# A bucketed attention with a Mish feed-forward layer on one core: float32 scores for the first 256 tokens alone, keys and values of the first head pairs in a buffer of their own, and a new order

## The chip, the core and the metric

The kernel runs on one core of a Trainium2 chip. The core has a matrix engine (PE, with its weight loads as PEld), a vector engine (DVE), a scalar engine (ACT), a general engine (POOL) and a queue engine (SP), which here issues every transfer. The engines run side by side, each through its own list of instructions in order, and wait for one another by semaphores. The metric is the device time of one execution in microseconds (us); less is better. A difference under about 0.3% (2.5 us) can't be told from none.

## The reference

For 4 batches of 8 heads, 768 tokens and 64 dimensions, queries and keys are hashed to 6 bits by the signs of a projection; a query attends only to keys of its own bucket. The 3,072 token rows of 512 channels then pass a feed-forward layer with h·tanh(softplus(h)).

```python
mask = q_bucket[:, :, :, None] == k_bucket[:, :, None, :]
scores = scale * np.matmul(q, k.transpose(0, 1, 3, 2))
scores = np.where(mask, scores, -1000000000.0)
attn = np.exp(scores - np.max(scores, axis=-1, keepdims=True))
attn = attn / (np.sum(attn, axis=-1, keepdims=True) + 1e-09)
...
h = x @ w_in
g = h * np.tanh(np.where(h > 20.0, h, np.log1p(np.exp(np.minimum(h, 20.0)))))
out = g @ w_out
```

The inputs of the feed-forward layer's weights are float64 and are brought to float32 on the chip from their bits.

## The kernel before

**Groups and slots.** The work is cut into 12 groups of 256 tokens (the code's `u`): batch 0 is groups 0, 1 and 2. A group has 8 slots (`n`), two for each of its 4 head pairs (`j`); a slot is 128 queries of a pair, both heads. A group also has 8 blocks `H`/`O` of the feed-forward layer. `BACKBONE` (L224) gives the order of the large steps on PE: S (scores of a slot), V (attention times values), H (first feed-forward product), O (second). The feed-forward layer runs three blocks of four slots behind the attention, so the first 12 slots stand largely before the first H.

**Two ways to a score.** In most slots the operands are float16 in two parts, high and low, with the hash bits beside the low part: `pe` (L933), 8 matmuls of float16 in a slot (line L937). This needs `q_prep` (L879) and `k_prep` (L786), which split a tensor (`k_hi`, `k_cp`, `k_lo` in the order's words), transpose both parts by a DMA through SP (L472), form hash bits with small PE products (L739), a sum (L743) and compares (L748). The other way is float32: `pe32` (L944, line L948) multiplies float32 halves on 64 rows each and adds bfloat16 hash bits. It needs `q_prep32` (L774) and `k_prep32` (L761): a transpose on PE (`turn32`, L450, with a copy at L453) and a product with the signed projection (`hash32`, L461, with a compare at L464). No DMA transpose and no splitting is needed for it.

**Who takes which.** `NF = 2` and `F32U = 3` (L219, L220): pairs 0 and 1 of groups 0, 1 and 2 take float32, that is 12 slots; the keys of pairs 0 and 1 of batch 0 are never split. All else takes float16. In group 0 the probabilities are transposed by PE (`pe_turn`, L434, copied by ACT at L437 or DVE at L438) and multiplied with raw float32 values (L1062), and its feed-forward blocks are float32 too (L1120, L1169).

**Memory.** The raw keys and values of batch 0 lie where other things will be: pairs 0 and 1 in the weights' tile `wi` (words 3072 to 6143), the values of pair 2 in the first slot of the ring `hl`, the keys of pairs 2 and 3 in `PT` (`kv_place`, L676). The ring `hl` holds normalised probabilities in two parts before their transposition. The weight pieces pass `w_prep` (conversion from float64 bits, L594 to L607) and `w_split` (into two float16 parts).

**What sets the order.** The operations are recorded in a plan, each with the engines that can do it; the table `ORDER` lists the plan's numbers with a letter for the engine chosen. Each engine's list is what falls to it from this table, so that a transfer that SP waits for holds up those behind it, and DVE, ACT and POOL do the softmax steps and the preparation steps in one fixed sequence: `max` at L978, scale at L961/L968, `exp` at L991, the row sum's reciprocal at L1021, `hi`/`lo` parts at L390 to L415.

Of the kernel before, what the change touches and what calls it, by code (L numbers as in the profile page):

```python
# [8 lines left out]
F16 = mybir.dt.float16  # L9
# [9 lines left out]
P = 128  # L19
# [8 lines left out]

# [59 lines left out]
137 7 9 8 50 20 0 5 11 19 12 22 1 2 3 4 76 80 29 81b 13 37 6 77b 14 15 10 25 33 26 30b 38 17 27 28 18 34 39 52  # L94
60 61 35 62 41 56 54 63 57 55 21 42 48 51 53 24 23 31 78 36 32 64 65 16 86 91 138 92 79 87 147 40 88 82 117 83
43 118 44 119b 93 89 66 109 110 111 153 90 94 120 67 112 154b 132 107d 46 108 133 113 95 115 68 114 116 124
125b 155 121 126 101 84 45 134 136 135 156 127b 178 96 128 140b 148 141 47 58 149 85 122d 123 97 99 142 139b
98b 143 129 168d 179 180d 100 174 176 69 175 177 170 130 157 171b 131 172 173b 204 205b 169 70 145b 182 189
144b 102 158 159 181 161b 190b 71 193 291 194 195 185 191 150 186 192 220 221 103 222d 183b 187 206 160b 196
188 197 104 223 212 152 146 49 151 162 59 105 106 213b 207 216 218 217b 219b 214 215b 184 353 224 243 163 239  # L100
164 244 245b 241 248 240 242 233c 270 368 307 210d 208 235 254 236 255 249 209b 237 246 238 247 225 256 271
250 257 234 272d 262 263 268 266 292 198 273 226 267b 211 227 293 165 294 269 251 283 284 349 350 264 303 265
285 295 166 304b 354 305 296 258 199 200 309d 286b 310 311c 260c 261 306 274 281 313 253 252 232 228 282 312b
322 201 317 364 287 365 288 289 290 366 318 319 355b 323 324 308 320 321 367 330b 331 315 338 339 72 231 203
202 167 229 397 369b 314 329 316 325 297 298b 275 276b 340 333 341 230 332b 334 342 73 370d 299 336 425c 277
74 426 371 399 378 379 380 335 328 302 400 398 300 373 424 423 351 337 301 280 381 427 372b 374 382 389c 411
376 259 375 278 279 406 429 458 428 390 412 452 407 352 391 383 384b 393 392c 395 326 327 385 453 408d 409 410
# [118 lines left out]

# [1119 lines left out]
```

## Time and profile before

| | us |
|---|---|
| median of 3 runs | 818.18 (816.49 to 818.43) |
| span of the profiled execution, first to last instruction | 815.4 |
| PE busy | 798.2 |
| DVE busy | 602.9 |
| ACT busy | 624.9 |
| POOL busy | 426.9 |

The span of the profiled execution lies 2.8 us under the median: a run's time has a start and an end around the span. The sums of the prediction are made on the span and carried to the median unchanged. [...]

### The profile page before, as it was taken

The page shows a single profiled execution, that of the slowest core. Times are in us where ns is not written, and L with a number is a line of the kernel's source. Part 1 is how long each engine was busy: PE and PEld are TensorE (multiplying, and loading weights), DVE is VectorE, ACT ScalarE, POOL GpSimd, SP SyncE. Part 2 cuts the span into 40 slices and gives each one's busy share as a digit, 9 for nine tenths or more (in the row PEclk, how much of TensorE's full clock was granted, in tenths as well). Part 3 has the DMA queues.
Part 4 walks back from the last instruction along what each step waited for, and adds up shares of the span by engine and source line. Part 5 has one row for each costly group of instructions (what it writes and reads, how often), then busy time and mean ns, then how long its engine had stood idle before and what let it go on. Part 6 is the DMA issues. An engine that isn't in the chain of part 4 may idle for free.

```text
span 815.4 us, 17000 instructions
## 1 busy us (share of the span) xinstructions
PE 798.2 (98%) x6546; PEld 549.6 (67%) x6546; DVE 602.9 (74%) x1103; ACT 624.9 (77%) x976; POOL 426.9 (52%) x434
## 2 busy tenths in 40 slices
PE   8899999999999999999999999999999999999998
PEld 5556666666676776676666676667676676776674
DVE  5888999988898778887887767768877675566211
ACT  4889998888696769889679698989779785677211
POOL 3564446554356773733585564344646758845120
PEclk9999999999999999999999999999999999999999
DMA  7958998989999969989989959999989577466200
GB/s 253 219 174 221 240 246 196 191 156 206 217 160 182 203 116 181 170 158 216 185 172 155 195 117 151 197 213 192 167 140 169 107 139 145 81 124 133 50 27 27
DMA packets 395489, 134.29 MB, mean 165 GB/s; under 512 B 365456, under 2 KB 386448, under 8 KB 395408
## 3 DMA queue, kind: packets, MB, share of 16 engines
q1 hardware_dynamic: 395408, 133.21, 81.2%
q8 instruction: 51, 0.84, 0.4%
q14 instruction: 30, 0.25, 0.1%
HBM read 35.65 MB, written 6.29 MB: 51 GB/s over the span
## 4 chain that ended last, share of the span: by engine, by line
PE 47%; ACT 1%; DVE 1%; DMA 1%; issue 0%; POOL 0%; SPq 0%; ACTq 0%; DVEq 0%
PE ps_s L937 7%; PE ps_o L1179 6%; PE ps_o L1181 6%; PE ps_o L1180 6%; PE ps_acc L1130 5%; PE ps_t L1088 5%; PE ps_acc L1132 5%; PE ps_acc L1131 5%; ACT pb L991 1%; DVE svb L978 1%; DMA out_dram<-ffb 1%; PE ps_t L739 0%; ACT L1315 0%; DVE hl L408 0%; ACT tok L480 0%
## 5 line engine op out<-in xcount | busy, mean ns | idle before, releaser
L991 ACT ACTIVATE pb<-ps_s,svb 128x768 f32<-128x768 f32 x184 | 180.9, 987 | 87.4 <-DVE svb L968 36.7
L978 DVE TENSOR_REDUCE svb<-ps_s 128x2 f32<-128x1536 f32 x92 | 161.3, 1753 | 40.2 <-PE ps_s L937 33.7
L1130 PE MATMUL ps_acc<-X,wo 128*128 128x256 f16 x616 | 167.9, 273 | 0.3 <-ACT ffb L1151 0.3
L1132 PE MATMUL ps_acc<-X,wo 128*128 128x256 f16 x616 | 167.9, 273 | 0.0
L1131 PE MATMUL ps_acc<-X,wo 128*128 128x256 f16 x616 | 167.9, 273 | 0.0
L1315 ACT ACT_TABLE_LOAD x117 | 150.1, 1283 | 2.0
L408 DVE SCALAR_TENSOR_TENSOR hl<-pb,svb,hl 128x768 f16<-128x768 f32 x131 | 140.3, 1078 | 13.8 <-POOL hl L390 9.8
L1181 PE MATMUL ps_o<-wi,ffb 128*128 128x512 f16 x352 | 133.4, 379 | 0.0
L1180 PE MATMUL ps_o<-wi,ffb 128*128 128x512 f16 x352 | 133.4, 379 | 0.0
L1179 PE MATMUL ps_o<-wi,ffb 128*128 128x512 f16 x352 | 133.4, 379 | 0.0
L937 PE MATMUL ps_s<-KT,QT 128*128 128x512 f16 (+1 forms) x656 | 120.1, 326 | 2.1 <-ACT pb L991 1.8
L390 POOL TENSOR_SCALAR hl<-pb,svb 128x768 f16<-128x768 f32 x68 | 71.0, 1046 | 75.9 <-DVE svb L1021 28.8
L937 PEld LDWEIGHTS <-QT 128*128 128x128 f16 x672 | 64.2, 98 | 40.5 <-issue 8.3
L1088 PE MATMUL ps_t<-PT,VT 128*64 128x256 f16 x1584 | 90.7, 273 | 0.0
L1088 PEld LDWEIGHTS <-VT 128*64 128x64 f16 x1584 | 84.8, 110 | 8.1 <-issue 7.6
L1151 ACT ACTIVATE ffb<-ps_acc,smalls 128x512 f32<-128x512 f32 x88 | 58.5, 684 | 33.5 <-PE ps_acc L1132 32.0
L415 POOL TENSOR_TENSOR hl<-pb,hl 128x768 f16<-128x768 f32 x45 | 75.0, 1667 | 3.8
L414 POOL TENSOR_SCALAR pb<-pb,svb 128x768 f32<-128x768 f32 x45 | 44.4, 987 | 48.0 <-ACT hl L392 21.4
L1131 PEld LDWEIGHTS <-wo 128*128 128x128 f16 x616 | 60.2, 98 | 13.3 <-issue 1.5
L1130 PEld LDWEIGHTS <-wo 128*128 128x128 f16 x616 | 60.2, 98 | 12.6 <-issue 0.5
L1132 PEld LDWEIGHTS <-wo 128*128 128x128 f16 x616 | 60.2, 98 | 7.0
L1181 PEld LDWEIGHTS <-ffb 128*128 128x128 f16 x352 | 34.4, 98 | 41.6
(240 smaller groups left out, 1300.5 us busy)
## 6 DMA issues: line engine op xcount, KB each, us to landing
out_dram<-ffb SPq DMA_DIRECT2D x22, 256.0 KB, 2.7
stg<-in_v_dram SPq DMA_DIRECT2D x13, 384.0 KB, 4.0
stg<-in_k_dram SPq DMA_DIRECT2D x12, 384.0 KB, 4.0
wo<-in_q_dram SPq DMA_DIRECT2D x9, 512.0 KB, 4.9
stg<-in_moe_w_in_dram SPq DMA_DIRECT2D x8, 512.0 KB, 4.6
stg<-in_moe_w_out_dram SPq DMA_DIRECT2D x6, 512.0 KB, 4.6
PT<-hl SPq DMA_TRANSPOSE x176, 4.1
wo<-in_moe_w_out_dram SPq DMA_DIRECT2D x5, 512.0 KB, 4.7
```

What stands on the lines that cost most here:

```text
L408: return [("DVE", 215 + 1.035 * n, port(lambda: nc.vector.scalar_tensor_tensor(out=dst, in0=src, scalar=sc, in1=hi, op0=ALU.mult, op1=ALU. ...
L937: nc.tensor.matmul(ps[:, hh * S + c0 * P:hh * S + c1 * P], QTb[:, u % 2, sl, qi], KTb[:, j, sl, hh * NCH + c0:hh * NCH + c1].rearrange("p ...
L978: op("max", [("DVE", 1755, lambda: nc.vector.tensor_reduce(out=sv[:, 0], in_=ps.rearrange("p (h e) -> p h e", e=S), axis=AX.X, op=ALU.max, ...
L991: EXP[n, hh] = op("exp", [("ACT", 1075, lambda hh=hh, t=t: nc.scalar.activation(pb[:, t], HOMES[n][0][:, hh * S:(hh + 1) * S], AF.Exp, bia ...
L1088: nc.tensor.matmul(pv[hh * D:(hh + 1) * D, y * 256:(y + 1) * 256], vt[:, w, hh * NCH + c], pt[:, hh, a * NCH + c].rearrange("p s t -> p (s ...
L1130: nc.tensor.matmul(o, wh, X[:, 0, c], start=(c == 0), stop=False)
L1131: nc.tensor.matmul(o, wh, X[:, 1, c], start=False, stop=False)
L1132: nc.tensor.matmul(o, wl, X[:, 0, c], start=False, stop=(c == NCC - 1))
L1179: nc.tensor.matmul(PS[f"o{s}"], gh, wh, start=first, stop=False)
L1180: nc.tensor.matmul(PS[f"o{s}"], gh, wl, start=False, stop=False)
L1181: nc.tensor.matmul(PS[f"o{s}"], gl, wh, start=False, stop=last)
L1315: for fn in plan.ordered("exp", lambda x: nc.scalar.preload_act_table_set(sets[x])):
```

## The change

`F32U` becomes 1: only group 0 takes float32 scores for its pairs 0 and 1 (4 slots instead of 12). So groups 1 and 2 drop `q_prep32`, and their `q_prep` takes all 16 blocks of 64 columns instead of 8. The keys of pairs 0 and 1 of batch 0 are now split as well: the two lines at L1241 that record `kv_stat(0, j, True)` and `k_prep(0, j)` at slots 1 and 3 come to life. Group 1 takes its pairs in the order 2, 3, 0, 1 (`turned`, L914). A new tile `ext` of 3,840 words holds the raw keys and values of pairs 0 and 1 and the values of pair 2; its room comes from the scratch for transfers, which is set to 1,024 bytes a partition. The tile `X` is laid out with the parts inside the channel blocks. The table `ORDER` is replaced as a whole: 2,655 operations instead of 2,636.

```diff
-F32U = 3
+F32U = 1
...
+    ext = cp.tile([P, 10 * S // 2], F32, name="ext")
...
-    Xb = ring("X", 2, [2, NCC, 256], F16)
+    Xb = ring("X", 2, [NCC, 2, 256], F16)
...
         if b == 0 and j < 2:
-            return [("wi", 3072 + (2 * j + x) * NKV, 3072 + (2 * j + x + 1) * NKV) for x in range(2)]
+            return [("ext", (2 * j + x) * NKV, (2 * j + x + 1) * NKV) for x in range(2)]
         if b == 0:
-            return [("pt1", (j - 2) * NKV, (j - 1) * NKV), ("hl", 0, NKV) if j == 2 else (SPARE[0], SPARE[1], SPARE[1] + NKV)]
+            return [("pt1", (j - 2) * NKV, (j - 1) * NKV), ("ext", 4 * NKV, 5 * NKV) if j == 2 else (SPARE[0], SPARE[1], SPARE[1] + NKV)]
...
-    nc = _bacc.Bacc("TRN2", target_bir_lowering=False, num_devices=1)
+    nc = _bacc.Bacc("TRN2", target_bir_lowering=False, num_devices=1, dynamic_dma_scratch_size=1024)
```

The first lines of the table, which say little by themselves:

```diff
-137 7 9 8 50 20 0 5 11 19 12 22 1 2 3 4 76 80 29 81b 13 37 6 77b 14 15 10 25 33 26 30b 38 17 27 28 18 34 39 52
...
+149 7 9 0 20 22 19 11 12 1 2 3 33 29 13 37 25 52 60 5 6 34b 18 30b 17 26b 10 14 35 38 15 27 61 36 62 54 50 31 28
```

PE at the first slot of group 1, before (ps_s: scores; QT, KT: transposed queries and keys; ps_l, ps_t: banks for transposes; X: raw queries):

```order
L948 LDWEIGHTS QT
L948 MATMUL ps_s<-KT,QT 128x512
L948 LDWEIGHTS QT
L948 MATMUL ps_s<-KT,QT 128x256
L948 LDWEIGHTS QT
L948 MATMUL ps_s<-KT,QT 128x256
L434 MATMUL ps_l<-ffb,pb 128x128 x3
L450 MATMUL ps_t<-ffb,X 64x128 x8
L434 MATMUL ps_l<-ffb,pb 128x128 x3
```

The same place on PE now (the line numbers of the changed kernel are 7 lower here; L930 is the float16 score, L427 the transpose of probabilities):

```order
L930 LDWEIGHTS QT
L930 MATMUL ps_s<-KT,QT 128x256
L930 LDWEIGHTS QT
L930 MATMUL ps_s<-KT,QT 128x512
L930 LDWEIGHTS QT
L930 MATMUL ps_s<-KT,QT 128x512
L427 MATMUL ps_l<-ffb,pb 128x128 x3
L427 MATMUL ps_t<-ffb,pb 128x128 x3
L427 MATMUL ps_l<-ffb,pb 128x128 x3
```

The score is float16, and the transposition of the next queries (L450) is gone from behind it.

DVE in group 0, around the fourth score maximum, before (svb: softmax scalars; hsum: hash sums; wo: where the split keys of pairs 2 and 3 stand before their transposition; PT: transposed probabilities):

```order
L743 TENSOR_REDUCE hsum<-ps_t 128x72
L748 TENSOR_SCALAR wo<-hsum 128x12x6
L743 TENSOR_REDUCE hsum<-ps_t 128x72
L978 TENSOR_REDUCE svb<-ps_b 128x2
L438 COPY PT<-ps_l 128x3x128 x2
```

The same stretch on DVE now (tok_64: where split keys or queries stand; L971 is the maximum, L386 and L401 the two parts of the split, L597 a part of the weights' conversion, L431 the copy of transposed probabilities):

```order
L386 TENSOR_SCALAR tok_64<-ext,smalls 128x12x64
L899 TENSOR_SCALAR smalls<-smalls 128x1
L401 SCALAR_TENSOR_TENSOR tok_64<-ext,smalls,tok_64 128x12x64
L736 TENSOR_REDUCE hsum<-ps_t 128x72
L431 COPY PT<-ps_l 128x3x128
L494 TENSOR_SCALAR smalls<-ps_t 128x4
L478 TENSOR_SCALAR smalls<-smalls 128x4
L971 TENSOR_REDUCE svb<-ps_b 128x2
L431 COPY PT<-ps_t 128x3x128
L597 TENSOR_SCALAR wi<-stg 128x1024
```

The split of a raw key tile from `ext` and a weight conversion stand between the softmax steps of group 0.

SP in group 0, before:

```order
L472 DMA_TRANSPOSE KT<-wo 128x12x128 x2
L472 DMA_TRANSPOSE QT<-tok_65 128x8x128
L468 DMA wi<-in_moe_w_in_dram 128x2x512
L472 DMA_TRANSPOSE KT<-wo 128x12x128
L468 DMA wo<-in_moe_w_in_dram 128x2x512
L472 DMA_TRANSPOSE KT<-wo 128x12x128
L468 DMA X<-in_q_dram 128x8x128
```

SP in the same place now:

```order
L465 DMA_TRANSPOSE KT<-wo 128x12x128
L465 DMA_TRANSPOSE QT<-tok_65 128x8x128
L465 DMA_TRANSPOSE KT<-tok_64 128x12x128
L465 DMA_TRANSPOSE KT<-wo 128x12x128
L461 DMA wo<-in_moe_w_in_dram 128x2x512
L465 DMA_TRANSPOSE KT<-tok_65 128x12x128
L461 DMA wi<-in_moe_w_in_dram 128x2x512
L465 DMA_TRANSPOSE KT<-wo 128x12x128
L465 DMA_TRANSPOSE QT<-tok_64 128x16x128
```

Two more key transposes (those of pair 0) stand among the others; those of pair 1 come later, among the transposes of `hl`.

## Rows read from the trace of the kernel before

**Rows 1.** The page: busy time by engine, and the granted TensorE clock.

```profile
PE 798.2 (98%) x6546; PEld 549.6 (67%) x6546; DVE 602.9 (74%) x1103; ACT 624.9 (77%) x976; POOL 426.9 (52%) x434
...
PEclk9999999999999999999999999999999999999999
```

**Rows 2.** Busy time by stretch: length, engines (instructions), clock, DMA share, GB/s.

```profile
core 0: us, PE busy (x) PEld busy (x) DVE busy (x) ACT busy (x) POOL busy (x), PEclk, DMA share, GB/s
0.00:73.85 73.85, 65.29 (x551) 43.23 (x552) 55.72 (x123) 55.94 (x112) 37.02 (x49) 1.00 0.78 217
73.85:198.36 124.51, 122.91 (x846) 84.92 (x846) 115.93 (x179) 113.50 (x168) 60.34 (x59) 1.00 0.96 204
198.36:815.40 617.04, 610.01 (x5153) 421.46 (x5151) 431.28 (x801) 455.50 (x698) 329.50 (x328) 1.00 0.79 151
6.74:73.85 67.11, 59.59 (x495) 37.71 (x492) 55.55 (x121) 54.36 (x109) 33.77 (x40) 1.00 0.79 219
...
80.00:160.00 80.00, 79.37 (x484) 52.96 (x483) 74.46 (x113) 72.01 (x110) 39.49 (x36) 1.00 0.97 219
```

**Rows 3.** Steps on PE in time order: start, length, engine, line, operation.

```profile
37.03 1.46 PE L937 MATMUL ps_s<-KT,QT 128*128 128x512 f16 x8
38.33 0.49 PE L434 MATMUL ps_l<-ffb,pb 128*128 128x128 f32 x3
...
56.01 2.25 PE L948 MATMUL ps_s<-KT,QT 64*128 64x256 f32 x15
58.18 0.55 PE L434 MATMUL ps_l<-ffb,pb 128*128 128x128 f32 x3
58.66 1.09 PE L450 MATMUL ps_t<-ffb,X 128*64 128x128 f32 x16
59.69 0.55 PE L434 MATMUL ps_l<-ffb,pb 128*128 128x128 f32 x3
...
86.78 1.02 PE L461 MATMUL ps_t<-QT,pw 128*128 128x512 f32 x2
87.84 0.38 PE L937 MATMUL ps_s<-KT,QT 128*128 128x512 f16 x1
```

**Rows 4.** PE by form: count, busy us, mean ns, idle before.

```profile
L739 PE MATMUL ps_t<-pj,KT 128*128 128x12 f16 x168 | 6.3, 168 | 1.2 <-DVE hl L408 0.7 <-DVE smalls L501 0.3 <-DMA KT<-tok 0.2
```

**Rows 5.** DVE by form, same columns.

```profile
L604 DVE TENSOR_SCALAR wi<-wi 128x1024 int32<-128x1024 int32 x1 | 0.7, 720 | 0.0
...
L438 DVE COPY PT<-ps_l 128x384 f32<-128x384 f32 x10 | 5.5, 554 | 3.4 <-PE ps_l L434 3.4
...
L393 DVE TENSOR_SCALAR tok<-stg,smalls 128x768 f16<-128x768 f32 x5 | 3.1, 619 | 0.3
...
L408 DVE SCALAR_TENSOR_TENSOR wo<-PT,smalls,wo 128x768 f16<-128x768 f32 x1 | 1.0, 1020 | 0.0
```

**Rows 6.** What DVE waited for from 0 to 74 us: total, times, longest.

```profile
DVE KT L453 <- PE ps_t L450: 5.8, 1, 5.8
DVE PT L438 <- PE ps_l L434: 3.4, 6, 1.2
DVE svb L978 <- PE ps_s L948: 2.2, 4, 0.9
DVE QT L464 <- PE ps_t L497: 1.3, 1, 1.3
```

**Rows 7.** What DVE waited for from 74 to 200 us.

```profile
DVE svb L978 <- PE ps_s L937: 1.8, 1, 1.8
DVE svb L978 <- PE ps_s L948: 1.7, 4, 0.7
```

**Rows 8.** Transfers: the page's queues, and issues with their time to landing.

```profile
q1 hardware_dynamic: 395408, 133.21, 81.2%
...
PT<-hl SPq DMA_TRANSPOSE x176, 4.1
...
KT<-tok SPq DMA_TRANSPOSE x24, 4.2
```

More of the change, by code (lines that the diff above doesn't have):

```diff
@@ L99 @@
[L99 to L103, printed above, removed]
@@ new lines @@
+1356 1525 1398 1534 1524b 1395c 1399 1401b 1500 1400 1472 1499 1501 1402 1440b 1529 1473 1482 1403 1511 1483
+1512c 1530 1514 1484c 1526 1513 1531d 1515 1533 1532 1474 1486 1538 1404 1547 1548 1539 1493 1475 1487 1516b
+1517 1826 1660 1427 1549c 1405 1557 1606 1502 1488 1518 1485 1551b 1558 1559c 1535 1550 1561 1560 1536c 1553
+1527 1489 1448c 1562d 1573 1528 1519b 1540b 1661 1574 1563 1406 1575c 1490b 1564b 1449b 1491b 1541 1503b 1566
+1662 1446c 1576 1700 1447b 1542 1577 1602 1603 1579c 1588 1555 1556 1570 1571 1616 1552 1589 1580 1590d 1554
@@ new lines @@
+1679b 1678 1680 1685 1686c 1687 1688 1689d 1690 1691c 1693b 1694 1711 1712 1713b 1704 1708 1715 1714 1681 1697
+1720 1739 1716 1692c 1695 1729 1705c 1668 1670 1730 1706 1731 1721 1669 1740 1741d 1696 1682b 1733 1743 1742
+1732b 1744d 1671 1709 1735 1745 1724 1734 1736 1887 1755 1717 1725 1718b 1727 1726 1746b 1710b 1756 1757 1758
+1748 1719 1698b 1759 1761d 1788 1784 1747c 1750 1762 1789 1785 1763 1770 1771 1772d 1749 1699 1857 1751 1737
+1798 1738 1765 1728 1774 1764b 1722 1723 1766 1773 1775d 1776 1777 1767 1830 1752 1786c 1831 1779 1793 1794
@@ L543, in hl @@
         return "hl", y * NKV + part * (NKV // 2), y * NKV + (part + 1) * (NKV // 2)
-    words = dict(hl=hl_w, stg=stg, ff=ff_w, wo=wo_w, wi=wi_w)
+    words = dict(hl=hl_w, stg=stg, ff=ff_w, wo=wo_w, wi=wi_w, ext=ext)
     def at(region):
@@ L702, in kv_stat @@
     def kv_stat(b, j, converted=False):
-        if j == 0 and not converted:
+        if b not in HKV:
             HKV[b] = small_ring("HKV", 2, [NPAIR, 2], I32)
@@ L1095, in att_pv @@
             i, o = j + y, pv[:, y * 256:(y + 1) * 256]
-            op("x_hi", [("ACT", 467, lambda i=i, o=o: nc.scalar.activation(X[:, 0, i], o, AF.Copy,
+            op("x_hi", [("ACT", 467, lambda i=i, o=o: nc.scalar.activation(X[:, i, 0], o, AF.Copy,
                                                                           scale=xf[:, i:i + 1]))],
@@ L1099, in att_pv @@
             op("x_lo", [("DVE", 483, lambda i=i, o=o: nc.vector.scalar_tensor_tensor(
-                out=X[:, 1, i], in0=o, scalar=xf[:, i:i + 1], in1=X[:, 0, i], op0=ALU.mult, op1=ALU.subtract))],
+                out=X[:, i, 1], in0=o, scalar=xf[:, i:i + 1], in1=X[:, i, 0], op0=ALU.mult, op1=ALU.subtract))],
                [pvn, xfn, (xn, i, i + 1)] + ([(f"{xn}l", j, i)] if y else []), [(f"{xn}l", i, i + 1)],
@@ L1129, in pe @@
                     wh, wl = hi[:, w:w + P], lo[:, w:w + P]
-                    nc.tensor.matmul(o, wh, X[:, 0, c], start=(c == 0), stop=False)
-                    nc.tensor.matmul(o, wh, X[:, 1, c], start=False, stop=False)
-                    nc.tensor.matmul(o, wl, X[:, 0, c], start=False, stop=(c == NCC - 1))
+                    nc.tensor.matmul(o, wh, X[:, c, 0], start=(c == 0), stop=False)
+                    nc.tensor.matmul(o, wh, X[:, c, 1], start=False, stop=False)
+                    nc.tensor.matmul(o, wl, X[:, c, 0], start=False, stop=(c == NCC - 1))
         xn = f"X{u % 2}"
```

218 lines of the change are left out of this document (106 added, 112 removed).

## The prediction

> **What bounds the kernel now.** [...] Then the busy times by stretch [rows 2], since the change touches only the first quarter. I cut at 73.85 us, where PE starts the first H block, and at 198.36, where it starts the score of slot 24, the first of batch 1; behind that point nothing is converted or scored in another form than before. From 198.36 on PE is busy for 610.0 of 617.0 us: whatever reaches slot 24 earlier ends earlier by as much. From 73.85 to 198.36 PE is busy for 122.9 of 124.5, but DVE already for 115.9 and ACT for 113.5. Before 73.85 no engine is full: PE 65.3, DVE 55.7, ACT 55.9 of 73.85, and DVE, from its first real work at 6.74 on, 55.55 of 67.11, a share of 0.83. So there are three stretches with three limits: a chain of short steps, three engines nearly level with PE ahead, and PE alone.
>
> **What the change takes from PE.** A float32 slot takes from 56.01 to 58.18, 2.17 us; a float16 slot from 37.03 to 38.33, 1.30 us [rows 3]. Eight slots change: 8 x 0.87 = 7.0 us. The query transposes of groups 1 and 2 fall away, 58.66 to 59.69, 1.03 us each, and so do their hash products, about 1.0 us each (1.06 from 86.78 to 87.84, with a small gap) [rows 3]: 4.1 us. Added are hash products of 12 matmuls for each of two key pairs and 8 more for each of two query groups, 40 in all; 168 of them cost 6.3 us of PE [rows 4], so 40 x 0.0375 = 1.5 us. Two small statistics add 0.1. The sum is -7.0 - 4.1 + 1.5 + 0.1 = -9.5 us. By stretch: before the first H stand 3 of the 8 slots, both transposes, one hash product and 20 of the 40 matmuls, -2.6 - 2.1 - 1.0 + 0.8 = -4.9; from there to slot 24 the rest, -4.6; behind slot 24 nothing.
>
> **What it gives to the other engines.** By the order of the changed kernel, DVE does in front of the product that completes group 0's attention: two more low parts of keys (L408, 1.02 us), two more high parts (L393, 0.62), three more pieces of weight conversion that POOL or ACT did (L604, 0.72) and three more copies of transposed probabilities (L438, 0.55) [rows 5], that is 2.0 + 1.2 + 2.2 + 1.7 = 7.1; the small ones (statistics, sums, scalars) less the compares and copies that fall away come to +0.7 by my count, at 0.15 to 0.6 us each. So DVE has 7.8 us more to do in the first stretch. In the second stretch its count changes by -0.9 (five low parts and three high parts of probabilities fewer, six weight parts more, and small ones), but some 1.7 us of it slipped from the first stretch to behind the last step that H needs: +0.8. ACT's count changes by less than 1.5 us in either, with two more squares and fewer copies and hash copies. POOL is half idle and stays so. SP gets four key transposes and longer query transposes; a transpose lands some 4 us after its issue [rows 8], and behind them in SP's queue wait weight loads and the transposes of `hl`. I cost that at nothing: the first use of the converted pairs is slot 12, which starts at 87.84 us now [rows 3], and what hides the transposes of pair 0 is the attention of slots 4 to 11. That cover is thin for pair 1 alone (rival 4); if it is gone, one landing of 4.1 us is paid. The new buffer costs no work: it lets SP load some weights earlier, into words that held raw keys, and I count no gain for it, since PE is busy for 0.987 of the stretch in which the weights are used first [rows 2].
>
> [...]
>
> **First stretch, term 1.** PE alone would make it 4.9 us shorter. But DVE must do 55.55 + 7.8 = 63.35 us after its start at 6.74. Bounds: if all of DVE's idle time stays (11.6 us), the first H comes 7.8 us later; if DVE kept pace with whatever PE sends, 4.9 us earlier. Much of the idle time is waiting for PE, 3.4 us for transposes, 2.2 for scores, 1.3 for a statistic [rows 6], and a leaner PE shortens some of it. The nearest row for a DVE that has enough to do is 80 to 160 us: 74.46 of 80.00, a share of 0.93 [rows 2]. At that share 63.35 us take 68.0, and 6.74 + 68.0 = 74.8: **+0.9 us** against 73.85.
>
> **Second stretch, term 2.** PE alone: 124.5 - 4.6 = 119.9 us, so -4.6. DVE has 115.9 + 0.8 = 116.7 to do. Its idle time is 124.5 - 115.9 = 8.6 us; 3.5 us of it are two waits for scores [rows 7], which end sooner when PE's scores are shorter; with the other 5.1 left DVE needs 121.8, so -2.7. At its old share of 0.93 it would need 125.4, +0.9. I take the middle between PE's end and DVE's with the score waits gone, **-3.6 us**, because in this stretch PE shows that the fullest engine can be busy for 0.987 of the time (122.9 of 124.5), which DVE would come near to. So the change gives PE room, and DVE becomes the one that is late next.
>
> **Third stretch, term 3.** Nothing: 0.
>
> Sum: +0.9 - 3.6 = -2.7 us. On the span 815.4 - 2.7 = 812.7; on the median 818.2 - 2.7 = **815.5 us**. The case's own range is 812.5 to 817.5.
>
> **The rivals.**
>
> Rival 1, PE's saving passes in full. It would be so if DVE's extra work before the first H only fills its idle time. For it: 11.6 us are idle there, more than 7.8; PE's rate is the bound behind 198 us. Against: a share of 63.35 / (67.11 - 4.9) = 1.02 would be needed of DVE, so part of that work would have to slip behind. 818.2 - 9.5 = 808.7.
>
> Rival 2, nothing is gained. [...] But where DVE's share in the first stretch reaches only 0.88, the first H comes at 6.74 + 72.0 = 78.7, +4.9, and with -3.6 the sum is +1.3; at 0.90 it is -0.3. Time: 818.2 + 0.5 = 818.7. [...]
>
> Rival 3, slower. DVE becomes the bound of group 0: its waits for transposes and row sums belong to a chain (score, maximum, exponential, transpose, copy) and do not shrink, and each added split delays the copy or maximum behind it, on which PE's next transpose waits. The price is the whole 7.8 us in the first stretch, with the -3.6 of the second kept: 818.2 + 4.2 = 822.4. It makes the kernel slower from the point where DVE's share in the first stretch falls under 0.896 (63.35 in 67.11 + 3.6), and by more than can be mistaken from 0.865 downwards; before, the share was 0.83, which speaks for it. Against it speaks that PE sends its steps earlier.
>
> Rival 4, the keys of pair 1 come late. Their second transposes stand on SP among the transposes of `hl` shortly before slot 14 needs them. One transpose that PE waits out is 4.1 us [rows 8]: 815.5 + 4.1 = 819.6.
>
> **How the numbers follow.** Forecast 0.40, rival 1 0.18, rival 2 0.18, rival 3 0.16, rival 4 0.08. A measurement of this kernel can tell about 0.3%, 2.5 us, from no change: faster means under 815.7, slower over 820.6. Faster: rival 1, 0.24 of the forecast's 0.40 (its range straddles 815.7) and 0.03 of rival 2, 0.45. Slower: rival 3, 0.02 of rival 2, 0.02 of rival 4, 0.20. Within: the rest, 0.35. The range takes in rival 1 and stops short of rival 3's worse half: 808.5 to 822.0.
>
> **What would show it.** In the profile of the changed kernel: the float16 slots of group 1 stand 1.30 us apart from their next step, and PE's busy time falls by some 9 us. The first H starts at 74 to 76 us; earlier than 71 speaks for rival 1, later than 78 for rival 3. DVE is busy for 0.92 or more of the time from 7 us to the first H. Slot 24 starts near 195.7. From slot 24 to the end it takes 617 us, as now; if that differs by more than 2 us, term 3 is wrong and the new order does something there that I did not see. A wait of PE for a transposed key in front of slots 12 to 15 is rival 4. The prediction is wrong in its core if DVE is not the fullest engine in front of slot 24.

## The result, and the profile after

The changed kernel takes 825.42 us (median of 4 runs, 825.02 to 828.39) against 817.58 us for the kernel before on the same chip: 1.0104 times as long, 95% interval 1.0085 to 1.0123. It is slower, where 815.5 was forecast with a range up to 822.0. The profiled execution's span is 823.3 us against 815.4.

The page of the changed kernel, busy times and clock, as in [rows 1]:

```profile
PE 794.4 (96%) x6498; PEld 545.3 (66%) x6498; DVE 629.9 (77%) x1195; ACT 613.6 (75%) x959; POOL 385.3 (47%) x386
...
PEclk9999999899999999999999999999999999999999
```

The three stretches of [rows 2], cut at the same steps (first H at 71.13, slot 24 at 200.63), and DVE's share up to the first H:

```profile
0.00:71.13 71.13, 62.33 (x518) 39.99 (x519) 59.78 (x140) 55.36 (x108) 36.46 (x48) 0.98 0.94 245
71.13:200.63 129.50, 120.74 (x829) 83.74 (x828) 118.10 (x183) 114.11 (x175) 60.76 (x61) 0.97 0.98 208
200.63:823.30 622.67, 611.37 (x5153) 421.61 (x5151) 452.03 (x875) 444.12 (x678) 288.07 (x277) 1.00 0.79 149
6.74:71.13 64.39, 57.32 (x462) 35.46 (x458) 58.26 (x132) 53.80 (x106) 32.54 (x38) 0.97 0.96 249
```

The first stretch is 2.7 us shorter than before, the second 5.0 longer, the third 5.6 longer: +7.9. To see where PE lost it, I took the length of every step on PE (its start to the start of the next step) less the shortest length of its kind in the traces (float16 score 1.30, float32 score 2.18, H 3.45 or 2.62, O 1.72 or 1.29, V 4.05 or 2.74, and so on). What is left over is idle time and time at a lower clock. The sum of the shortest lengths is what PE would need with nothing in its way: 784.5 us before, 774.6 after. The table shows what is lost on top, by stretch in us of the profile; each row is one execution, and the last three kernels are explained below.

| kernel | 0-73 | 73-118 | 118-155 | 155-262 | 262-400 | 400-580 | 580-end |
|---|---|---|---|---|---|---|---|
| before | 13.9 | 1.3 | 0.8 | 4.4 | 2.2 | 2.2 | 1.3 |
| changed | 16.3 | 2.2 | 10.5 | 1.5 | 2.8 | 8.6 | 2.0 |
| w_behind_xhi | 14.7 | 2.3 | 5.9 | 1.8 | 2.9 | 9.5 | 1.9 |
| old_tail | 17.2 | 2.0 | 10.7 | 1.9 | 3.8 | 2.3 | 1.3 |
| old_from_s16 | 14.7 | 2.3 | 5.2 | 4.8 | 3.1 | 1.9 | 1.3 |

So the change takes 9.9 us of work from PE, as counted, and PE loses 18 us more than before, at two places: near 118 to 155 us and from 400 to 580 us.

**The first place.** The two longest waits of PE from 118 to 153 us in the changed kernel (total, times, longest); in the kernel before no wait is listed there:

```profile
PE ps_t L489 <- ACT stg L473: 4.8, 1, 4.8
PE ps_s L930 <- ACT pb L984: 3.5, 4, 1.2
```

The first line is a statistic of the last weight piece (L489, a small matmul with a tile of ones), the second the scores, which wait for the exponentials of the slot before. The list of SP, ACT, DVE and PE in time order (start, length, line, operation, idle time before and what ended it) shows how the statistic came to wait. SP issues the load of the piece's raw words in two halves of 512 KB, at 133.35 and 135.01:

```profile
133.35 0.34 SPq L461 DMA_DIRECT2D stg<-in_moe_w_out_dram  x1
135.01 0.34 SPq L461 DMA_DIRECT2D stg<-in_moe_w_out_dram  x1
```

The transfers themselves took 3.7 and 5.7 us from issue to landing:

```profile
stg<-in_moe_w_out_dram SPq DMA_DIRECT2D x1, 512.0 KB, 3.7
stg<-in_moe_w_out_dram SPq DMA_DIRECT2D x1, 512.0 KB, 5.7
```

What SP waited for before these two issues is the piece ahead, which still held the room in `stg`:

```profile
SPq L461 <- DVE wi L600: 2.6, 1, 2.6
SPq L461 <- ACT stg L473: 1.2, 1, 1.2
```

ACT, which needs those words at L587:

```profile
138.23 0.46 ACT L1089 ACTIVATE X<-ps_t,smalls 128x256 f16<-128x256 f32 x1
140.76 1.15 ACT L587 ACTIVATE stg<-stg 128x1024 f32<-128x1024 f32 x1 [2.07 <-DMA stg<-in_moe_w_out_dram]
141.79 1.14 ACT L594 ACTIVATE wo<-stg 128x1024 int32<-128x1024 uint16 x1
142.82 0.47 ACT L1089 ACTIVATE X<-ps_t,smalls 128x256 f16<-128x256 f32 x1
146.03 0.99 ACT L984 ACTIVATE pb<-ps_s,svb 128x768 f32<-128x768 f32 x1 [2.74 <-DVE svb L961]
147.18 1.06 ACT L473 ACTIVATE stg<-wo 128x1024 bf16<-128x1024 f32 x1
```

DVE:

```profile
143.33 0.48 DVE L1092 SCALAR_TENSOR_TENSOR X<-ps_t,smalls,X 128x256 f16<-128x256 f32 x1 [4.79 <-ACT X L1089]
143.73 1.75 DVE L971 TENSOR_REDUCE svb<-ps_s 128x2 f32<-128x1536 f32 x1
```

PE:

```profile
136.98 1.46 PE L930 MATMUL ps_s<-KT,QT 128*128 128x512 f16 x8 [0.58 <-ACT pb L984]
138.27 3.62 PE L1113 MATMUL ps_acc<-X,wi 128*128 128x256 f32 x16
141.73 1.88 PE L1162 MATMUL ps_o<-wo,ffb 128*128 128x512 f32 x4
148.38 0.17 PE L489 MATMUL ps_t<-smalls,ones 128*128 128x4 bf16 x1 [4.77 <-ACT stg L473]
149.35 2.72 PE L930 MATMUL ps_s<-KT,QT 128*128 128x512 f16 x8 [0.78 <-ACT pb L984]
```

Read from the top. The second half of the load is issued at 135.01, and ACT can use the words at 140.76. The two `x_hi` on ACT (L1089) and the two `x_lo` on DVE (L1092) bring the high and low parts of the product V6 out of its bank. ACT's instruction that waits for the words stands between the two `x_hi`, so the second `x_hi` ends only at 143.29. DVE's first `x_lo` (L1092) needs only the first `x_hi`, done at 138.69, but starts when the second is done. Behind it in DVE's list stands the maximum of slot 18 (L971), whose scores had been ready since 138.3. It starts at 143.73; the exponential follows at 146.03, behind that the square of the weight piece (147.18), and PE's statistic, which stands in PE's list ahead of slot 19, waits until 148.38. After 4.8 us in which PE did next to nothing its granted clock falls (0.64 on average from 148.4 to 156 us): the score of slot 19 takes 2.51 us from its start to the next step instead of 1.30, and the O step behind it 2.72 instead of 1.72.

Why the first `x_lo` waits for the second `x_hi` as well, 4.79 us on DVE, no run here shows.

**The second place.** The longest of PE's waits from 400 to 580 us in the changed kernel; before, one wait of 0.3 us is listed there:

```profile
PE ps_s L930 <- ACT pb L984: 3.2, 6, 0.9
PE ps_t L732 <- DVE X L1092: 1.4, 1, 1.4
PE ps_acc L1123 <- ACT ffb L1144: 0.8, 2, 0.5
```

These are many small waits, most of them again for the exponentials.

### The profile page after: what moved, and what is told of

It is laid out like the page before. It is cut to its first block, busy times and chain, and to the rows that moved or that the text cites. A ratio compares the mean times of both kernels' runs of the same rounds, so it can differ in the third digit from the quotient of the medians.

```text
span 823.3 us, 16983 instructions
## 1 busy us (share of the span) xinstructions
PE 794.4 (96%) x6498; PEld 545.3 (66%) x6498; DVE 629.9 (77%) x1195; ACT 613.6 (75%) x959; POOL 385.3 (47%) x386
## 5 line engine op out<-in xcount | busy, mean ns | idle before, releaser
L971 DVE TENSOR_REDUCE svb<-ps_s 128x2 f32<-128x1536 f32 x92 | 161.2, 1752 | 25.6 <-PE ps_s L930 22.4
L930 PE MATMUL ps_s<-KT,QT 128*128 128x512 f16 (+1 forms) x720 | 134.2, 330 | 8.3 <-ACT pb L984 8.2
L401 DVE SCALAR_TENSOR_TENSOR hl<-pb,svb,hl 128x768 f16<-128x768 f32 x127 | 133.7, 1058 | 8.7 <-POOL hl L383 4.7
L930 PEld LDWEIGHTS <-QT 128*128 128x128 f16 x736 | 70.9, 98 | 52.6 <-issue 17.1
L383 POOL TENSOR_SCALAR hl<-pb,svb 128x768 f16<-128x768 f32 x60 | 63.4, 1057 | 90.2 <-DVE svb L1014 37.1
L407 POOL TENSOR_SCALAR pb<-pb,svb 128x768 f32<-128x768 f32 x49 | 49.2, 1004 | 73.4 <-ACT hl L385 41.0
L408 POOL TENSOR_TENSOR hl<-pb,hl 128x768 f16<-128x768 f32 x49 | 81.1, 1654 | 4.1
L385 ACT ACTIVATE hl<-pb,svb 128x768 f16<-128x768 f32 x60 | 55.5, 928 | 23.7 <-DMA PT<-hl 9.2
L1124 PEld LDWEIGHTS <-wo 128*128 128x128 f16 x616 | 60.2, 98 | 14.1 <-issue 2.1
L1123 PEld LDWEIGHTS <-wo 128*128 128x128 f16 x616 | 60.2, 98 | 12.9 <-issue 0.4
L401 DVE SCALAR_TENSOR_TENSOR ffb<-ffb,smalls 128x512 f16<-128x512 f32 x64 | 51.0, 801 | 21.7 <-POOL ffb L383 18.7
```

The source lines that it names most:

```text
L401: return [("DVE", 215 + 1.035 * n, port(lambda: nc.vector.scalar_tensor_tensor(out=dst, in0=src, scalar=sc, in1=hi, op0=ALU.mult, op1=ALU. ...
L930: nc.tensor.matmul(ps[:, hh * S + c0 * P:hh * S + c1 * P], QTb[:, u % 2, sl, qi], KTb[:, j, sl, hh * NCH + c0:hh * NCH + c1].rearrange("p ...
L971: op("max", [("DVE", 1755, lambda: nc.vector.tensor_reduce(out=sv[:, 0], in_=ps.rearrange("p (h e) -> p h e", e=S), axis=AX.X, op=ALU.max, ...
L1123: nc.tensor.matmul(o, wh, X[:, c, 0], start=(c == 0), stop=False)
L1124: nc.tensor.matmul(o, wh, X[:, c, 1], start=False, stop=False)
```

## The experiments

Three theories stood at the start. **Theory 1**: the new order puts instructions that wait in front of work that the next slot needs, at the two places. **Theory 2**: DVE, with more work than before, is the bound. **Theory 3**: the changed memory places cost the time. All results, as ratio to the kernel before on the same chip:

| run | median us | ratio | 95% interval |
|---|---|---|---|
| old_calc_new_mem | 817.57 | 1.0010 | 1.0000 to 1.0019 |
| old_tail | 819.37 | 1.0026 | 1.0013 to 1.0038 |
| old_from_s16 | 815.75 | 0.9986 | 0.9972 to 1.0000 |
| old_from_s16_again | 816.88 | 0.9998 | 0.9985 to 1.0011 |
| w_behind_xhi | 822.17 | 1.0076 | 1.0051 to 1.0101 |
| stat_behind_s19 | 823.44 | 1.0081 | 1.0064 to 1.0098 |
| three_moves | 819.52 | 1.0029 | 1.0015 to 1.0044 |
| spaced | 819.13 | 1.0026 | 1.0013 to 1.0039 |
| half_early | 816.54 | 0.9999 | 0.9987 to 1.0011 |
| dve_relief | 833.38 | 1.0197 | 1.0167 to 1.0227 |
| dve_less | 816.13 | 0.9990 | 0.9974 to 1.0007 |
| max_first | 826.94 | 1.0103 | 1.0070 to 1.0135 |
| tail_repaired | 825.60 | 1.0098 | 1.0076 to 1.0121 |
| both_repaired | 821.20 | 1.0055 | 1.0037 to 1.0073 |
| kept_busy | 818.00 | 1.0012 | 1.0002 to 1.0021 |
| after_kept_busy | 827.48 | 1.0128 | 1.0114 to 1.0142 |

### Memory, order or computation

**old_calc_new_mem**: the old computation and order on the new memory places.

```diff
-F32U = 1
+F32U = 3
-ORDER of the changed kernel
+ORDER of the kernel before
```

> The old computation (float32 scores for all three groups of 256 tokens) in the old order, on the new memory places: the extra tile for raw keys and values, the layout of X by column block, and the transfer scratch of 1,024 bytes. Theories 1 and 2 (the places cost nothing): 816.5 to 819 us, ratio to the kernel before within 0.3%. Theory 3 (the places cost the time): 822 to 826 us. A gain of up to 1 us would show that they free an early load.

817.57 us, ratio 1.0010. Theory 3 falls: in the old order the extra tile, the layout of `X` and the smaller scratch cost at most 1.6 us together (the upper end of the interval).

**old_tail** and **old_from_s16**: the changed kernel up to the scores of one slot, then the same operations in the order of the kernel before.

```diff
 ORDER of the changed kernel up to the scores of slot 40 (old_tail) or 16 (old_from_s16)
-the rest in the order of the changed kernel
+the rest in the order of the kernel before
```

> The changed kernel as it is up to the scores of slot 40 (about 319 us), and from there on the same work in the order of the kernel before. The stall near 118 to 153 us is left in. Theory 1 (the new order itself loses some 6.5 us between 400 and 580 us, since the maximum starts later behind the scores there, and PE waits for the exponentials): this comes back, 818 to 820.5 us, and the time between the marks of slot 48 and slot 72 falls from 194.0 to about 188 us. Theory 3 (changed memory places) or a cost of the computation itself: nothing comes back, 824 to 827 us.

> The changed kernel up to the scores of slot 16 (near 122 us); from there on the same remaining work in the order of the kernel before, still with float16 scores. Theory 1 (the loss is in the order of the changed kernel behind slot 16, at two places): the stretch 118 to 155 us loses about 1 to 3 us over the shortest step times instead of 10.5, and 400 to 580 us about 2 instead of 8.6: 812 to 816 us, faster than the kernel before by 0.1 to 0.6%. Rival (the front part leaves the weight pieces and VectorE late, so that any order behind it would wait): the stretch 118 to 155 us still loses 6 to 10 us, and only the later part comes back: 818 to 820 us.

old_tail takes 819.37 us and old_from_s16 815.75, so 9.7 us of the changed kernel's 825.42 lie in the order behind slot 16 (8.5 by the second measurement of that kernel, below). "Order" means here the sequence and the choice of engines together; no run separates the two. Busy time from 400 to 580 us (columns as in [rows 2]), in the changed kernel:

```profile
400.00:580.00 180.00, 174.32 (x1476) 120.05 (x1475) 142.64 (x270) 141.90 (x211) 89.68 (x95) 1.00 0.87 166
```

and in old_tail:

```profile
400.00:580.00 180.00, 179.29 (x1516) 123.88 (x1515) 138.53 (x256) 154.53 (x236) 101.87 (x102) 1.00 0.92 173
```

PE's idle time there falls from 5.7 to 0.7 us. The new order also gives DVE 4 us more in this stretch, and ACT and POOL 12 to 13 us each less. Both expectations of theory 1 came true in size, old_from_s16 at the edge of its range, and the rival for old_from_s16, that the new front leaves everything behind it late, did not: its stretch 118 to 155 us loses 5.2 us, not 10.5. Yet 5.2 is more than the 1 to 3 I had expected.

**old_from_s16_again** is the same kernel once more, on another chip.

> The kernel of old_from_s16 once more, beside half_early on the same chip and with more executions: 815 to 816.5 us, ratio to the kernel before 0.997 to 1.000, so that it can be told whether the new computation with the old order behind slot 16 beats the kernel before.

816.88 us, ratio 0.9998: the ratio lies in the expected range, the time 0.4 us over it and outside the 812 to 816 us first expected. With the order behind slot 16 out of the way the new computation is level with the kernel before: the 9.9 us that PE saves are given back elsewhere. The table of losses says where: 4.4 us more than before at 118 to 155, and about 1 us each in front of 73, from 73 to 118 and from 262 to 400. Its row is an execution at a granted clock of 1.00 (814.34 us); the middle execution lies some 2 us over it.

### The first place

**w_behind_xhi**: two ACT instructions of the weight piece come behind the second `x_hi` (547 and 549 are the two `x_hi`; 523 and 524 are `w_u` and `w_low`, the instructions at L587 and L594).

```diff
-546 522 521 547 523 524b 549 562 564 609
+546 522 521 547 549 523 524b 562 564 609
```

> The changed kernel with two ScalarE instructions of the last weight piece (w_u at L587, w_low at L594) put behind the second x_hi of V6 instead of in front of it; all else is as in the changed kernel. Theory 1 (the new order put a wait for a late weight load in front of work that slot 18 needs): ScalarE no longer waits 2.1 us between the two x_hi, VectorE's first x_lo no longer waits 4.8 us, the maximum of slot 18 starts near 139.5 us instead of 143.7; PE's statistic in front of slot 19 still waits for the square of that piece, so only a part comes back: 820 to 823.5 us. Theory 2 (VectorE is the bound there, or the loss is spread over the whole kernel): nothing comes back, 824.5 to 826.5 us. Theory 3 (the changed memory places cost it): as theory 2.

822.17 us, within the expectation of theory 1. What DVE waited for from 125 to 150 us is now:

```profile
DVE wo L597 <- ACT wo L591: 1.1, 1, 1.1
DVE X L1089 <- ACT X L1086: 0.5, 1, 0.5
```

The wait for `x_hi` has gone from 4.8 to 0.5 us, PE's wait for the statistic from 4.8 to 1.6, and slot 24 follows slot 12 by 110.9 us instead of 115.5. The stall also stands in the profiles of four later kernels that keep this place as it is (old_tail, max_first, tail_repaired and after_kept_busy: PE waits 3.9 to 4.4 us for the statistic, and slot 24 follows slot 12 by 114.8 to 115.5 us). In the medians the gain is only 2.3 us (0.28% of 817) where the profiles show 4.6, and the interval overlaps that of the changed kernel; the executions of this kernel spread from 820.4 to 826.8. The clearer pair is tail_repaired and both_repaired, below, which differ by this move alone and ran on one chip: 825.60 against 821.20 us, with intervals that do not overlap. PE's wait for the statistic in the one and in the other:

```profile
PE ps_t L486 <- ACT stg L470: 4.1, 1, 4.1
PE ps_t L486 <- ACT stg L470: 1.0, 1, 1.0
```

So the chain read above is the cause of the long stall.

**stat_behind_s19** and **three_moves** go on from there: the statistic too moves behind slot 19, with the square behind both exponentials (the first) or where it was (the second, which also takes the old order from slot 40 on).

```diff
-612 526 613 578 577 606 527 631 570 528
+612 613 526 578 577 606 631 570
...
-599 622 601b 608
+599 622 527 601b 608 528
```

> As the run before, and moreover ScalarE's square of the last weight piece (L473) is put behind the second exponential of slot 18, and PE's statistic of that piece (L489) with VectorE's reading of it behind the scores of slot 19 and the two O steps that follow. Theory 1: PE's idle stretch of 4.8 us at 143.6 is gone, and with it the lower clock that followed (slot 19 at 2.51 us instead of 1.30, the next O step at 2.72 instead of 1.72): 6 to 7 us less than the changed kernel, 818 to 820 us. If the clock falls for another reason, the lower part of that: 820 to 821.5 us. Theories 2 and 3: 824.5 to 826.5 us.

> w_behind_xhi with PE's statistic of the last weight piece and VectorE's reading of it behind the scores of slot 19 and the two O steps that follow (the square stays where it was), and from slot 40 on the order of the kernel before. If the three losses add up: 822.2 less 1.6 to 3 for the statistic's wait less 5.5 to 6.5 for the part behind slot 40: 813 to 816 us, at or a little under the kernel before. If the statistic's wait is only handed on to the next step, as in stat_behind_s19: 816 to 817.5 us. If the moves do not add up: over 818 us.

Neither gained: 823.44 us lies between the ranges of its theories, and 819.52 us, level with old_tail alone, in the one for moves that do not add up. The statistic no longer waits, but in stat_behind_s19 an O step then waits 1.5 us and the stretch 155 to 200 us loses 3.5 us instead of 0.6. PE's wait for the statistic was a symptom; what is behind it in the lists is just as late.

**spaced** and **half_early**, on old_from_s16: more PE work between the scores of slots 15 to 17, and DVE's reading of a statistic (459), for which V6 waited 1.9 us, put earlier; half_early makes the second move alone.

```diff
 spaced: H6 605, +O40 565, S16 552, O50 571, +O41 566, +O51 600, S17 572, V6 546
 both:   max 513, mb 514, +half 459
```

> old_from_s16 (815.75 us) with PE's list altered around slots 15 to 18: one more O step between the scores of slots 15 and 16, two more between 16 and 17 (the scores stood 4.8 us of PE work apart there, while score, maximum and both exponentials of one slot take about 6 us), and VectorE's reading of the statistic of weight piece 11, for which the value step waited 1.9 us, put right behind the maximum of slot 15. Theory (the losses of that stretch are waits for a chain that the work between is too short to cover): the stretch 118 to 155 us loses 2 to 3 us instead of 5.2, 812.5 to 814.5 us. Rival (VectorE or the transposes are the bound of that stretch, PE's idle time only moves to the value step): 815 to 816.5 us.

> old_from_s16 with one VectorE instruction moved: the reading of the statistic of weight piece 11 goes from behind the maximum of slot 17 to behind the scaling of slot 15, since it keeps the bank that V6 needs and V6 waited 1.9 us for it. Theory: V6 starts 0.7 to 1.9 us earlier (then the transposes of slot 15 are what it waits for), 814 to 815.5 us. Rival (what follows V6 waits for VectorE anyway): as old_from_s16.

819.13 us, 2 to 3 us worse and over both ranges, and 816.54 us, the same. In `spaced` V6 waits 1.0 us for a transpose of probabilities, and slot 19 2.6 us for exponentials; in `half_early` V6 no longer waits for DVE, but 2.2 us for a transpose instead. The idle time of PE is not removed by filling it. The slots stand 6 us apart there (15 to 17 at 115.1, 121.2, 127.1 us in old_from_s16; before, 113.7, 120.5, 128.2), and the score waits for the exponentials of the slot before. One slot's score, maximum, scaling and two exponentials take about 6 us at these slots (in the changed kernel from 116.64 to 122.57 us for slot 16 and from 122.71 to 128.49 for slot 17). A float16 score shortens PE's part of that chain by 0.9 us and no other part (one maximum took 1.75 us and one exponential 0.99 in the kernel before and in the changed one). That this chain is what spaces the slots is read from the waits; no run shortens the chain, so it is not shown.

### Is DVE the bound?

**dve_relief**: on w_behind_xhi, six roundings or extractions between slots 8 and 15 go from DVE to POOL.

```diff
-335c 391c 367c 473c 464c 444c
+335b 391b 367 473 464b 444
```

> w_behind_xhi (822.2 us) with six roundings or low-bit extractions between slots 8 and 15 (three of the attention rows, three of weights) moved from VectorE to GpSimd, on which they take 0.9 to 1.2 us: about 4.0 us of VectorE's work is taken out of the stretch 60 to 118 us, where it was busy 97% or more. If VectorE is what ends that stretch: slot 15 starts 2.5 to 4 us earlier than in w_behind_xhi (near 112 instead of 115.5 us) and the time is 818.5 to 820.5 us. If the slots there are tied to the chain of score, maximum and exponential, or to PE: slot 15 within 1 us, 821.5 to 823 us. If GpSimd's longer instructions come into the chains: later and slower, 823 to 826 us.

833.38 us, slower than all three ranges. POOL around 76 us (time order), and what ACT and PE waited for from 70 to 95 us:

```profile
76.48 2.80 POOL L380 TENSOR_SCALAR stg<-wi,smalls 128x1024 f16<-128x1024 f32 x1 [2.18 <-DVE smalls L475]
79.28 0.29 POOL L962 TENSOR_SCALAR svb<-svb,smalls 128x2 f32<-128x2 f32 x1
```

```profile
ACT pb L981 <- POOL svb L963: 5.2, 1, 5.2
PE ps_s L927 <- ACT pb L981: 4.0, 1, 4.0
```

One moved rounding waits 2.18 us for DVE and then takes 2.80 us, and the scaling of slot 10 (L962) stands behind it in POOL's list: ACT waits 5.2 us, PE 4.0. The same mechanism as at the first place, on a third engine; as a test of theory 2 it settles nothing. A rounding of the same size, of another piece, took 1.12 us on POOL at 89.25 us of w_behind_xhi. Why the one took 2.80 us and the other 1.12 was not shown.

**dve_less**: on old_from_s16, four low halves of weights between slots 12 and 16 are set to zero instead of computed.

```diff
+LESS = ((1, 0), (0, 1), (1, 1), (0, 2))
...
+        if x in LESS:
+            low[0] = ("DVE", 300, lambda: nc.vector.memset(lo, 0.0))
```

> old_from_s16 (815.75 us) with the low halves of four weight pieces (both halves of w_in and w_out that the first group uses next) set to zero on VectorE instead of computed, so that four instructions of 1.27 us between slots 12 and 16 become four of about 0.3 us: 3.9 us of VectorE's work is left out there, and that part of the computation. If VectorE is the bound of the stretch 73 to 118 us, where it is 97% busy: slot 16 starts 2.5 to 4 us earlier relative to slot 12 (37.5 us after it before), and the time is 811.5 to 813.5 us. If PE is the bound there (its list loses 2.3 us in that stretch): slot 16 within 1 us, 815 to 816.5 us.

816.13 us. Busy time from 73 to 118 us in old_from_s16:

```profile
73.00:118.00 45.00, 44.99 (x269) 31.37 (x268) 43.37 (x62) 42.93 (x66) 23.81 (x24) 1.00 1.09 257
```

and in dve_less:

```profile
73.00:118.00 45.00, 45.00 (x267) 31.38 (x267) 40.14 (x62) 42.47 (x66) 22.99 (x23) 1.00 1.10 256
```

DVE loses 3.2 us of work (the four instructions that set to zero took 0.48 us each), and slot 16 still stands 37.5 us behind slot 12 in both. An engine that was busy for 96% of the stretch was not its bound; PE, busy for all of it, is the one left. Theory 2 falls for that stretch. For the time in front of 73 us and from 118 to 155 us no run settles it.

### The second place

**max_first**: in the changed kernel, at slots 52, 62, 64, 66 and 70 the maximum goes in front of the DVE instruction ahead of it (at 62 and 66 an `x_lo` that waits for `x_hi`). Three of the five moves:

```diff
-1726 ... 1756 1757      -1808 ... 1853      -1779 ... 1794 1795b
+1756 1757 1726          +1853 1808          +1794 1795b 1779
```

> The changed kernel with VectorE's list altered at five slots of the later part, 52, 62, 64, 66 and 70: the maximum of the slot goes in front of the one instruction that stood ahead of it and ran or waited when the scores were done (an x_lo that waits for ScalarE's x_hi at 62 and 66, a rounding or remainder at 52, 64 and 70). All else is as in the changed kernel; the stall near 118 to 153 us stays. Theory: there the maximum started 1.2 to 2.2 us after the scores and PE then waited for the exponentials of these slots; with the maximum first, the stretch 400 to 580 us loses 4 to 6 us over the shortest step times instead of 8.6, and the time is 820.5 to 823 us. Rival (the lateness is only handed to the remainder, the transposes and the next value step): 824 to 826.5 us.

826.94 us, over the rival's range. The losses right behind slots 52 and 62 are gone (1.3 and 1.1 us), but PE loses 3.1 us at 523 us, where it lost 1.6. What DVE and ACT waited for from 516 to 526 us:

```profile
DVE smalls L865 <- ACT tok L470: 4.9, 1, 4.9
ACT tok L470 <- DMA KT<-tok: 2.6, 1, 2.6
```

ACT's square of the next queries waits for a transpose that still reads the tile, and DVE's reading of that square stands in front of the maximum of slot 66.

**tail_repaired** moves these two, with a small instruction that follows them (1860), behind, and **both_repaired** adds the move of w_behind_xhi.

```diff
-1858 ... 1807 1799 1809      -1859 ... 1860 ... 1853 1808 1845 1810
+1807 1799 1809 1858          +1853 1808 1845 1810 1859 1860
```

> max_first with one more place altered: ScalarE's square of the queries of group 9, which waits 2 to 2.6 us for a transpose that still reads the tile it writes, goes behind the two x_hi of V30, and VectorE's reading of it (own), for which VectorE waited 2.2 us in the changed kernel and 4.9 us in max_first in front of the maximum of slot 66, goes behind that maximum and the two x_lo. Theory (the losses at 400 to 580 us are, one by one, an instruction that waits for a late transfer or for another engine and stands in front of a slot's maximum or exponential): the stretch 400 to 580 us loses 4 to 5.5 us instead of 8.6 to 8.8, and PE's loss of 3.1 us at 523 us is gone: 821.5 to 824 us against 825.4 of the changed kernel and 826.9 of max_first. Rival (each repair hands the wait to the next chain): the stretch loses 8 us or more, 825 to 827.5 us.

> tail_repaired and the move of w_behind_xhi in one kernel, so the changed order repaired at both places by moves of single instructions. Theory: the gains add up, 817.5 to 821.5 us. Rival: as w_behind_xhi alone, 821.5 to 823.5 us.

825.60 us for the first: the rival. The time from slot 48 to slot 72 fell only from 194.0 us in the changed kernel to 192.9; in old_tail it is 189.1. From 520 to 530 us POOL and ACT now wait, and PE behind them:

```profile
POOL tok L380 <- DVE smalls L861: 4.0, 1, 4.0
PE ps_s L927 <- ACT pb L981: 3.1, 1, 3.1
ACT pb L981 <- POOL svb L963: 2.8, 1, 2.8
```

The rounding of the queries on POOL needs the value that DVE now reads later, and the scaling of slot 67 stands behind that rounding. Each repair of one list handed the wait to the next list. both_repaired takes 821.20 us, 4 us less than the changed kernel (ratio 1.0055 against 1.0104). That lies just inside the range in which the gains add up, but the interval reaches that of w_behind_xhi alone (1.0051 to 1.0101), so it is not shown that the moves at the second place gave anything in the total. It stays at or above old_tail (1.0026; the intervals just touch), which has the stall of the first place still in it. So the second place is shown to be the order as a whole (old_tail), and not shown to be any one instruction; by what single property the old order does better there stays open.

### The clock in front of 73 us

**kept_busy**, on old_from_s16, and **after_kept_busy**, on the changed kernel: small matmuls at five waits of PE between 18 and 33 us.

```diff
+    def keep_busy2(to):
+        for _ in range(6):
+            nc.tensor.matmul(to, ones, ones[:, 0:to.shape[1]], start=True, stop=True)
```

> old_from_s16 (815.75 us) with five groups of six small matmuls on the tile of ones (their results are not used) put in front of the five steps between 18 and 33 us at which PE waited 0.6 to 1.0 us each. Theory (the new front of the list leaves PE idle so often there that its granted clock falls in most executions, which the mean clock of 0.994 to 0.998 shows, while the executions at 1.000 took 813.5 to 814.3 us): mean clock 0.999 to 1.000, median 813.0 to 814.5 us, S4 near 34.3 us. Rival (the clock falls for another reason): clock as before, 815.5 to 817 us. If the small matmuls delay PE themselves: up to 1.5 us more at S4.

> The changed kernel itself (825.4 us) with the same five groups of small matmuls. Theory: the clock at 20 to 40 us no longer falls, 1.5 to 3 us less, 822.5 to 824 us, with the stalls behind slot 16 left as they are (the clock still falls once near 148 us after PE's idle stretch, mean clock 0.995 to 0.998). Rival: 825 to 826.5 us.

Both are slower, 818.00 and 827.48 us, outside the theory's and the rival's ranges. The changed kernel, without these matmuls, from 30 to 40 us:

```profile
30.00:35.00 5.00, 3.23 (x39) 1.99 (x38) 4.01 (x15) 3.18 (x6) 1.62 (x3) 0.94 0.90 188
35.00:40.00 5.00, 4.98 (x29) 2.82 (x28) 3.03 (x4) 3.24 (x9) 4.34 (x5) 0.72 1.19 254
```

kept_busy from 45 to 55 us:

```profile
45.00:50.00 5.00, 3.67 (x32) 2.47 (x33) 2.40 (x15) 3.19 (x7) 0.00 (x0) 0.74 0.97 331
50.00:55.00 5.00, 4.87 (x39) 3.40 (x39) 4.42 (x10) 4.58 (x7) 3.85 (x6) 0.92 0.86 188
```

The clock of 1.00 held up to 45 us in kept_busy and fell there instead, behind a wait of PE of 1.7 us for a late transpose. In after_kept_busy it held, though PE waited 1.4 us at the same place:

```profile
20.00:55.00 35.00, 29.68 (x277) 19.87 (x273) 30.46 (x74) 30.56 (x61) 15.86 (x24) 1.00 1.03 229
```

Yet that execution took 827.56 us. Its first H starts at 71.56 us, where two executions of the same front without the small matmuls, also at a clock of 1.00, have it at 69.56 and 69.57 (w_behind_xhi and old_from_s16): the small matmuls delay PE by 0.8 us up to slot 4 (35.06 against 34.26) and by 2.0 up to the first H, more than the lower clock took in the changed kernel, whose first H starts at 71.13. The theory that the five waits alone bring the clock down is not confirmed: the mean clock of kept_busy was 0.995 to 1.000 in eleven executions, and that of old_from_s16 0.993 to 1.000 in 21.

## Why the prediction was wrong, step by step

**PE's saving, -9.5 us: right.** The sum of the shortest lengths fell by 9.9. The float16 slots of group 1 take 1.31 us (slot 8 from 55.05 to 56.36). That PE's busy time would fall by 9 us did not come true (798.2 to 794.4): a matmul at the lower clock counts as busy for longer (the score of slot 19 above is recorded with 2.72 us, that of slot 18 with 1.46), and idle time grew, from 17.2 to 28.9 us.

**Term 1, +0.9: it was -2.7** (first H at 71.13). The mis-sized term is DVE's 7.8 us: up to the first H DVE did 59.78 us of work against 55.72, 4.1 more, and 1.4 of that stood in front of 6.74 us, from which the term counts. And the step from a share of DVE to a time was wrong in kind. DVE's share was 0.90 (58.26 of 64.39), not 0.92 or more, and dve_less shows, for 73 to 118 us, that a DVE busy for 0.96 of the time sets nothing there. Part of what was lost went with the lower clock. The same front at a clock of 1.00, in old_from_s16:

```profile
0.00:69.57 69.57, 60.91 (x518) 39.42 (x519) 60.01 (x140) 55.31 (x108) 36.51 (x48) 1.00 0.95 249
```

There the first H starts 4.3 us earlier than in the kernel before, close to the 4.9 that PE alone would give: in this stretch rival 1 was nearly right.

**Term 2, -3.6: it was +5.0.** This step failed. Its working put each engine's busy sum against the stretch and took the fuller one as the bound. What the runs showed in its place: neither sum was the bound (PE 120.7 and DVE 118.1 of 129.5 us). One ACT instruction that waited for a load in front of the work of slot 18 cost 4.6 us of it (slot 12 to slot 24, 115.5 against 110.9 us in w_behind_xhi). Without that stall the stretch still takes 125.0 us there (69.56 to 194.52), 0.5 more than before and 4 more than forecast. The reading for these 4 us is the chain of score, maximum and exponential, which float16 shortens by 0.9 us of 6 and which no busy sum contains; it was not tested, and so this part of the cause stays open. The prediction had named SP's queue and the weight loads behind the new transposes, and costed them at nothing because PE was 0.987 busy. A load was indeed the start of the stall, but not behind the new transposes: SP had issued the last key transpose at 102.3 us and the last query transpose at 115.1, and waited for DVE and ACT to free the load's room. Slot 24 at 194.5 us, with the stall gone, lies near the forecast's 195.7 by luck: the first stretch gains there what the second was to gain.

**Term 3, 0: it was +5.6.** The text named this sign: if the part behind slot 24 differed by more than 2 us, the new order did something there that I did not see. old_tail shows that it did. I had read the table as changed only where the computation changes; it is another order and another choice of engines to the end: against [rows 2] DVE has 20.7 us more behind slot 24, POOL 41.4 and ACT 11.4 less. Putting this term at nothing was the second step that failed; old_tail shows 6.0 us in its place (825.42 against 819.37), from the order behind slot 40 alone.

**The rivals.** Rival 3 had the sign and came nearest in time (822.4), but by luck: DVE did not become the bound of group 0, whose stretch got shorter. Rival 4: PE has no wait for transposed keys from 73 to 118 us. Rival 1 holds nearly up to slot 12, which started 2.7 us early, and 4.2 to 4.3 in the two executions at a clock of 1.00. Rival 2, nothing gained, is what the new computation gives with the old order behind slot 16 (0.9998), but not for its reason, a DVE that holds back the first H. By the prediction's last sentence it was wrong in its core: in front of slot 24 PE was the fullest engine (183.1 us against DVE's 177.9). No rival said that the new order itself could be worse than the old where the computation is the same.

## What to carry to other kernels

A table that replaces the order of a whole kernel is a change to the whole kernel: look at what stands in each engine's list right behind an instruction that waits for a transfer, also where the computation stays as it was. A sum of busy times does not give the time of a stretch: PE did 9.9 us less here and the time stayed, even in the better order. Ask also what the chain through a step is, and how long it takes. (That the chain is what took the gain here is likely, and not shown.) When a wait is found, move the instruction that waits behind everything that is due, on every engine that passes the value on. That repaired the first place; at the second, each move handed the wait to the next list, and only the other order as a whole helped.

## What the runs showed of the hardware

The granted clock differs between executions of one kernel. In the 106 executions of the kernel before that ran beside the experiments, the mean clock was 0.998 to 1.000; of 21 executions of old_from_s16, five at 1.000 took 813.5 to 815.3 us and seven at 0.993 to 0.996 took 815.6 to 820.3, the middle one 816.9. Of 16 profiles of kernels with the new front, ten show a lower clock in a stretch between 20 and 55 us (0.72 from 35 to 40 us in the changed kernel, where PE's listed waits from 13 to 41 us come to 4.0 us, against 3.0 in the kernel before), and four show 1.00 there (w_behind_xhi, old_from_s16, dve_less and after_kept_busy); of the other two, half_early and old_from_s16_again, the mean clock was 0.996 and 0.998. The kernel before shows 1.00 in every stretch from 13 to 55 us, and old_calc_new_mem a mean clock of 1.000. The middle one of the five at 1.000 is 814.9 us, of the other sixteen 816.9, so some 2 us of the new computation's lost gain go with the clock; what brings it down there was not found, and no remedy.

The two 512 KB halves of one weight piece landed 3.7 and 5.7 us after their issues at 133.35 and 135.01 us in the changed kernel (transfer engines 0.83 busy from 133.35 to 140.76). A rounding of 128 x 1024 values took 1.12 us on POOL at 89.25 us of w_behind_xhi, and another of the same size 2.80 us at 76.48 us of dve_relief.
